# A key-weight load moved to the second DMA queue at the start of a transformer block

## The chip, the cores and the metric

The kernel runs on one core of a Trainium2 chip. Runs e1 to e8 were made on one chip (number 5 in the record) and e9 to e12 on another (number 1); for the first comparison the record names none. Kernels are compared only within the same rounds. The time of a kernel is the device time of one execution in microseconds (us). Most of the time I use the span of the trace, from the first to the last instruction of the program. It is about 1.8 us shorter than the device time of the same execution.

## The reference

A pre-norm block of two halves on `x` of 2048 tokens by 1024 features, in bfloat16:

```
h  = x + LinearAttention(LayerNorm(x)) @ wo      # 32 heads of 32, phi(t) = elu(t)+1
h2 = h + TokenMLP(LayerNorm(h))                  # w1: 2048 -> 3584 tokens, gelu, w2 back
```

The change touches the very beginning only: layer norm of the first token tiles (128 tokens each, called x0, x1, x2, ...), their transposes, and the first products with the key part of `wqkv`.

## The kernel before

The kernel is already tuned, and TensorE (the matmul engine) is its limit: it is busy for 570.0 of 578.6 us. Loads come over two hardware DMA queues, one fed by the sync engine (SP) and one by ScalarE (ACT); nearly everything is on SP's (65.94 MB by the profile page, against 0.13 MB on ACT's). The key weights are loaded as two column blocks, and each block as two halves of 512 KB. "First half" and "second half" below are those of the first block.

```python
            def load_x(i, halves=False):
                x_sb = xload.tile([P, D], BF16, name="x_sb")
                if halves:
                    nc.sync.dma_start(x_sb[:, 0:CW], x[i * P:(i + 1) * P, 0:CW])
                    pin(nc.scalar.dma_start(x_sb[:, CW:D], x[i * P:(i + 1) * P, CW:D]))
                else:
                    nc.sync.dma_start(x_sb[:], x[i * P:(i + 1) * P, :])
                return x_sb
            # ... (cut)
            xs = {0: load_x(0, True)}
            xs[1] = load_x(1)
            for k0 in (0, hk):
                nc.sync.dma_start(wkv[:, k0:k0 + hk, 0:CW], wqkv_v[:, k0:k0 + hk, D:D + CW])
            nc.scalar.add_instruction(  # load of ScalarE's function table
                # ... (cut)
            )
            xs[2] = load_x(2)
            for k0 in (0, hk):
                nc.sync.dma_start(wkv[:, k0:k0 + hk, CW:D], wqkv_v[:, k0:k0 + hk, D + CW:2 * D])
            for i in range(3, G0 + 2):      # x3, x4, x5
                xs[i] = load_x(i)
            # ... the value and query weights follow (cut)
            warm_up(10)                     # matmuls on zeros
            # ... (cut)
            ln_stats(0)                     # VectorE: statistics of x0
            stats(0)                        # ScalarE: rstd of x0
            ln[1] = ln_chunks(1, xs.pop(1))
            pin(ln[1][1](0))                # VectorE: statistics of x1, first half
            norm_halves(0)                  # VectorE: norm of x0 ("norm 0")
            transpose_in(0)                 # TensorE transposes, ScalarE copies
            pin(ln[1][1](1))
            pin(ln[1][2]())
            stats(1)
            k_unit(0, 0)                    # TensorE: x0 times the first key block, 4 + 4 matmuls
            norm_halves(1)
            transpose_in(1)
            ln_stats(2)
            stats(2)
            k_unit(1, 0)
            norm_halves(2)
            # ... k_unit(0, 1) (cut)
            transpose_in(2)
            ln_stats(3)
            # ... rstd of x3 on ScalarE; more work on VectorE (cut)
            norm_halves(3)
            # ... k_unit(1, 1) on TensorE (cut)
            transpose_in(3)
```

`pin` keeps the order of an engine's list as written, and in the traces VectorE runs these instructions in that order. So statistics of x1 that wait for their load also hold up norm 0 behind them.

Of the kernel before, what the change touches and what calls it, by code (L numbers as in the profile page):

```python
# [27 lines left out]
def kernel(  # L28
# [12 lines left out]
    nc = tc.nc  # L41
    x = A_x.flatten_outer_dims()
    o_dram = out.flatten_outer_dims()
    S, D = x.shape
    F = B_w1.shape[1]
    NS, ND, NF = S // P, D // P, F // P
    CW = min(BANK, D)
# [35 lines left out]
    pin = tc.keep_in_program_order  # L83
# [253 lines left out]
    with ExitStack() as actx:  # L337
# [18 lines left out]
        wqkv_v = A_wqkv.rearrange("(k p) c -> p k c", p=P)  # L356
        wo_v = A_wo.rearrange("(k p) c -> p k c", p=P)

        with ExitStack() as a1:
            a1w = a1.enter_context(tc.tile_pool(name="a1w", bufs=1))  # L360
            wkv = a1w.tile([P, ND, 2 * D], BF16)
# [17 lines left out]
# [8 lines that stand above are left out]
# [258 lines left out]
            hk = max(1, ND // 2)  # L645
            assert NDC == 2 and G0 == 4 and ND % 2 == 0
            xs = {0: load_x(0, True)}
            xs[1] = load_x(1)
            for k0 in (0, hk):
                nc.sync.dma_start(wkv[:, k0:k0 + hk, 0:CW], wqkv_v[:, k0:k0 + hk, D:D + CW])  # L650
            nc.scalar.add_instruction(
                mybir.InstLoadActFuncSet(name=nc.get_next_instruction_name(), act_func_set_id=ACT_SET_LN_EXP, ins=[], outs=[])
            )
# [414 lines left out]
```

## Time and profile before

| | before |
|---|---|
| device time, first 3 runs | 579.37 us median (579.31 to 581.21) |
| span of the profiled run | 578.6 us |
| TensorE busy | 570.0 us (99%) |

The first lines of the profile page give the span and the busy time of each engine:

```profile
span 578.6 us, 7489 instructions
...
PE 570.0 (99%) x2832; PEld 267.5 (46%) x2854; DVE 385.6 (67%) x752; ACT 212.6 (37%) x433; POOL 1.8 (0%) x8
```

A table by stretches of time (start:end in us, then busy time and instructions of each engine, granted TensorE clock, DMA share, GB/s) shows where TensorE is not busy:

```profile
0.00:8.27 8.27, 5.30 (x18) 2.02 (x19) 4.61 (x26) 3.20 (x7) 1.83 (x8) 1.00 0.73 234
8.27:18.25 9.98, 8.74 (x55) 4.34 (x56) 7.03 (x17) 6.08 (x16) 0.00 (x0) 1.00 1.09 358
18.25:36.00 17.75, 17.54 (x96) 8.45 (x95) 15.45 (x33) 10.82 (x23) 0.00 (x0) 1.00 0.80 253
```

TensorE (PE) lacks 1.24 us between 8.27 and 18.25 us and 0.21 us in the next stretch. What comes after 18 us is one unbroken piece of matmul work. So the question is when that piece starts.

The timeline of the head (start, duration, engine, line, operation, and in brackets the idle time before it and what ended it):

```profile
5.02 0.64 DVE L396 BATCH_NORM_STATS2 st<-x_sb 128x6 f32<-128x512 bf16 x1
...
5.70 0.73 DVE L406 TENSOR_SCALAR xn<-x_sb,mv,rstd 128x512 bf16<-128x512 bf16 x2
...
6.17 0.85 PE L670 MATMUL tp<-ident,xn 128*128 128x128 bf16 x8 [0.53 <-DVE xn L406]
...
8.27 1.02 PE L427 MATMUL acc_t<-wkv,xnT 128*128 128x512 bf16 x4 [1.25 <-DMA wkv<-in_A_wqkv_dram]
...
9.67 1.02 PE L427 MATMUL acc_t<-wkv,xnT 128*128 128x512 bf16 x4 [0.37 <-DMA wkv<-in_A_wqkv_dram]
...
14.02 1.29 DVE L396 BATCH_NORM_STATS2 st<-x_sb 128x6 f32<-128x512 bf16 x2 [0.79 <-DMA x_sb<-in_A_x_dram]
...
17.28 0.73 DVE L406 TENSOR_SCALAR xn<-x_sb,mv,rstd 128x512 bf16<-128x512 bf16 x2
...
17.75 0.72 PE L670 MATMUL tp<-ident,xn 128*128 128x128 bf16 x8 [0.35 <-DVE xn L406]
```

Line 427 is the product with key weights, line 670 the transposes, line 396 the statistics, line 406 the norm. TensorE waits 1.25 us for the first half of the key weights and 0.37 us for the second. VectorE (DVE) waits 0.79 us for x3 and then works through to norm 3, which releases the transposes of x3 at 17.75 us. TensorE was idle 0.35 us before those. I call the start of these transposes the gate: from there on TensorE hardly waits.

The chain of work that ended last, followed back through the head, agrees: it goes from VectorE's statistics of x3 straight to the DMA of x3 (start, duration, what):

```profile
4.46 9.54 DMA x_sb<-in_A_x_dram
...
14.02 1.30 DVE st L396 x2
```

x3 was issued at 4.46 us and took 9.54 us to land.

### The profile page before, as it was taken

How to read it: one execution, taken by the hardware profiler on the slowest of the kernel's cores; microseconds unless marked ns; L12 is line 12 of the kernel's file. 1: busy time of each engine (PE TensorE's matmuls, PEld its weight loads, DVE VectorE, ACT ScalarE, POOL GpSimd, SP SyncE). 2: the span in 40 equal slices, each digit the busy share in tenths (PEclk: the TensorE clock that was granted, in tenths of full speed). 3: DMA queues.
4: the chain of work that ended last, by engine and by line, in shares of the span. 5: the costliest groups of instructions: out<-in, count | busy, mean ns of one | idle time of the engine just before them, and what ended most of it. 6: DMA issues, size and time to landing. Idle time of an engine off the chain costs nothing.

```text
span 578.6 us, 7489 instructions
## 1 busy us (share of the span) xinstructions
PE 570.0 (99%) x2832; PEld 267.5 (46%) x2854; DVE 385.6 (67%) x752; ACT 212.6 (37%) x433; POOL 1.8 (0%) x8
## 2 busy tenths in 40 slices
PE   7999999999999999999999999999999999999998
PEld 3444444455555444444444444444444444444444
DVE  5898888546767889876666666667765455456443
ACT  4647677666667777342222322222100000000000
POOL 1000000000000000000000000000000000000000
PEclk9999999999999999999999999999999999999999
DMA  8933331029437952152224422203976446431101
GB/s 288 359 81 74 83 81 37 19 88 286 83 73 154 293 171 94 55 146 73 74 72 114 104 74 72 74 0 88 221 218 159 118 126 172 129 99 46 36 28 36
DMA packets 109827, 66.55 MB, mean 115 GB/s; under 512 B 31826, under 2 KB 101728, under 8 KB 109792
## 3 DMA queue, kind: packets, MB, share of 16 engines
q1 hardware_dynamic: 109584, 65.94, 43.0%
q8 instruction: 22, 0.36, 0.3%
q14 instruction: 13, 0.11, 0.1%
q10 hardware_dynamic: 144, 0.13, 0.1%
q0 software_dynamic: 64, 0.01, 0.0%
HBM read 50.34 MB, written 8.39 MB: 102 GB/s over the span
## 4 chain that ended last, share of the span: by engine, by line
PE 93%; DMA 3%; DVE 2%; SPq 1%; issue 1%; ACT 0%; DVEq 0%
PE psZ L228 17%; PE psW L228 17%; PE psX L228 17%; PE acc_t L922 9%; PE acc_t L775 9%; PE psY L228 8%; PE psB L503 4%; PE psC L503 4%; PE psA L503 4%; PE psE L503 2%; DMA x_sb<-in_A_x_dram 2%; PE nd_ps L873 1%; DMA xr<-in_A_x_dram 1%; DVE wo_sb L477 1%; DVE st L396 0%
## 5 line engine op out<-in xcount | busy, mean ns | idle before, releaser
L228 PEld LDWEIGHTS <-sa 128*128 128x128 f16 x1134 | 110.4, 98 | 131.7
L223 DVE TENSOR_TENSOR sa<-w1p 128x1024 f16<-128x1024 bf16 x70 | 47.9, 685 | 20.0 <-PE psX L228 12.4
L775 PE MATMUL acc_t<-xnT,wq_sb 128*128 128x512 bf16 x248 | 57.3, 379 | 0.4
L922 PE MATMUL acc_t<-wo_sb,pqT 128*128 128x512 bf16 x250 | 55.7, 379 | 0.3
L223 DVE TENSOR_TENSOR sa<-w2p 128x1792 f16<-128x1792 bf16 x40 | 43.3, 1084 | 10.1 <-PE psW L228 7.6
L922 PEld LDWEIGHTS <-pqT 128*128 128x128 bf16 x256 | 24.8, 98 | 29.0
L775 PEld LDWEIGHTS <-wq_sb 128*128 128x128 bf16 x256 | 24.6, 98 | 27.4
L164 DVE TENSOR_SCALAR e_sb<-e_sb 128x512 bf16<-128x512 bf16 x64 | 18.5, 289 | 25.9 <-ACT e_sb L160 25.4
L264 DVE TENSOR_TENSOR tt<-psW,dd 128x512 f32<-128x512 f32 x22 | 15.2, 691 | 29.3 <-PE psW L228 29.2
L228 PEld LDWEIGHTS <-w2p 128*128 128x128 bf16 x224 | 21.9, 98 | 26.4
L228 PEld LDWEIGHTS <-w1p 128*128 128x128 bf16 x224 | 21.9, 98 | 26.4
L259 DVE TENSOR_TENSOR psY<-psX,dd 128x512 f32<-128x512 f32 x22 | 15.4, 699 | 27.5 <-PE psX L228 27.5
L160 ACT ACTIVATE e_sb<-acc_t 128x512 bf16<-128x512 f32 x40 | 23.9, 597 | 26.6 <-PE acc_t L775 23.7
L503 PEld LDWEIGHTS <-xs 128*128 128x128 f16 x208 | 20.0, 98 | 23.4 <-DVE xs L489 1.3
L269 DVE TENSOR_TENSOR tt<-tt,psZ 128x512 f32<-128x512 f32 x22 | 15.1, 688 | 18.0 <-PE psZ L228 17.9
L228 PE MATMUL psZ<-hT_2227,w1p 128*128 128x512 f16 x112 | 26.8, 379 | 0.0
L503 PE MATMUL psA<-wkv,xnT 128*128 128x512 bf16 x98 | 26.4, 379 | 0.3
L228 PE MATMUL psW<-hE,sa 128*128 128x512 f16 x112 | 26.6, 379 | 0.0
L228 PE MATMUL psX<-hT_2226,sa 128*128 128x512 f16 x112 | 26.6, 379 | 0.0
L228 PE MATMUL psX<-hO,sa 128*128 128x512 f16 x112 | 26.5, 379 | 0.0
L228 PE MATMUL psW<-hT_2228,w1p 128*128 128x512 f16 x112 | 26.5, 379 | 0.0
L228 PE MATMUL psZ<-hO,sa 128*128 128x512 f16 x112 | 26.5, 379 | 0.0
(258 smaller groups left out, 839.5 us busy)
## 6 DMA issues: line engine op xcount, KB each, us to landing
w1p<-in_B_w_dram SPq DMA_DIRECT2D x14, 1024.0 KB, 5.7
w2p<-in_B_w_dram SPq DMA_DIRECT2D x8, 1792.0 KB, 8.6
xr<-in_A_x_dram SPq DMA_DIRECT2D x16, 256.0 KB, 3.6
x_sb<-in_A_x_dram SPq DMA_DIRECT2D x15, 256.0 KB, 3.0
wkv<-in_A_wqkv_dram SPq DMA_DIRECT2D x4, 512.0 KB, 8.1
wkv<-in_A_wqkv_dram SPq DMA_DIRECT2D x2, 1024.0 KB, 10.0
wq_sb<-in_A_wqkv_dram SPq DMA_DIRECT2D x2, 1024.0 KB, 12.3
wo_sb<-in_A_wo_dram SPq DMA_DIRECT2D x2, 1024.0 KB, 6.6
```

What stands on the lines that cost most here:

```text
L160: pin(nc.scalar.activation(e_sb[:], src, ACT.Exp))
L164: pin(nc.vector.tensor_scalar(e_sb[:], e_sb[:], 1.0, PHI_EPS, ALU.min, ALU.add))
L223: return nc.vector.tensor_tensor(t, a, b, op)
L228: nc.tensor.matmul(ps[:, cols], lhsT=sa[:, k, :], rhs=mv(k)[:, cols], start=(start and k == 0), stop=(stop and k == self.nk - 1), skip_gro ...
L259: nc.vector.tensor_tensor(self.Y[:], self.X[:], self.d[:], ALU.add)
L264: nc.vector.tensor_tensor(self.t[:], self.W[:], self.d[:], ALU.add)
L269: nc.vector.tensor_tensor(self.t[:], self.t[:], self.Z[:], ALU.subtract)
L477: pin(nc.vector.tensor_tensor(out, a, b, ALU.subtract))
L503: pin(nc.tensor.matmul(ps[:], lhsT=lhs[:, k, :], rhs=rhs[:, k, :], start=(start and k == 0), stop=(k == hk2 - 1), skip_group_check=True,))
L775: nc.tensor.matmul(qp[:, 0:SW], lhsT=wq_sb[:, kt, j * P:(j + 1) * P], rhs=xnT[:, kt, u * SW:(u + 1) * SW], start=(kt == 0), stop=(kt == ND ...
L873: nc.tensor.matmul(nd_ps[:, b, sl * NCOL:(sl + 1) * NCOL], lhsT=pqT[:, j, i * P:(i + 1) * P], rhs=ndrhs[:, j, :], start=True, stop=True,)
L922: nc.tensor.matmul(ap_[:, 0:CW], lhsT=pqT[:, j, i * P:(i + 1) * P], rhs=wo_sb[:, j, dc * CW:(dc + 1) * CW], start=(j == 0 and not SEED_RES ...
```

## The change

The intent is to have the first half of the key weights travel beside x1 instead of behind it, so that the first key matmul does not wait. No instruction is added or removed; TensorE's and VectorE's lists stay in the same order.

```diff
             xs[1] = load_x(1)
-            for k0 in (0, hk):
-                nc.sync.dma_start(wkv[:, k0:k0 + hk, 0:CW], wqkv_v[:, k0:k0 + hk, D:D + CW])
+            pin(nc.scalar.dma_start(wkv[:, 0:hk, 0:CW], wqkv_v[:, 0:hk, D:D + CW]))
+            nc.sync.dma_start(wkv[:, hk:ND, 0:CW], wqkv_v[:, hk:ND, D:D + CW])
```

## The prediction

> **What bounds the kernel now.** The page has TensorE busy for 570.0 of 578.6 us (99%). By a table of stretches it is busy 5.30 of the first 8.27 us, 8.74 of the next 9.98, 17.54 of the 17.75 up to 36.0 and over 99% after that; the view of waits lists 0.3 and 0.2 us for it after 18 us. So the kernel ends as much earlier as TensorE reaches its unbroken stretch (from 17.75 us) earlier.
>
> **The head of the kernel (timeline, landing events).** x0 lands at 3.6 to 3.7 us, x1 at 4.6, the first key half block at 8.15, the second at 9.6, x2 at 10.3, x3 at 14.0. TensorE waits 1.2 us for the first half (starts 8.27; ScalarE has copied the transposed x0 at 7.89, its first half at 7.35) and 0.4 us for the second (9.67). VectorE waits 0.8 us for x3, then works without a gap to the end of norm 3 (17.69), which releases the transposes of x3 at 17.75 after 0.35 us of TensorE idle. That is the last gate. Of the first half's 16 engine shares, 15 land by 6.54 us, one at 8.14: one DMA engine took 1.09 us for one 1 KB packet at 4.64, just after its x1 share, and stays 1.4 us behind in every later load (x3: 15 shares by 12.62, the last at 13.99). From 4.0 to 4.5 us the DMA engines moved 59 KB, against 175 KB per half us later.
>
> **What the change does.** No work is added or removed; TensorE's and VectorE's orders stay. ScalarE's queue gets one issue (0.4 to 0.5 us) ahead of its table load (1.28 us); its first real work is at 5.14, so this is free. The sync queue's later issues move forward 0.43 us.
>
> [...] As an estimate from the steady 350 GB/s, x1 shares with at most its own 256 KB of weights and lands up to 0.7 us later, at 4.7 to 5.3. VectorE asks for it at 5.02, ahead of norm 0, so 0 to 0.3 us may be lost there. The first half lands at 6.5 to 7.5, the second at 7.5 to 9. The first key matmul moves from 8.27 to about 7.5, and the 1.6 us of waits for key weights mostly go.
>
> **What reaches the end.** The bytes ahead of x3 are the same, and x3 gates norm 3. x3 gains the 0.1 to 0.4 us by which the slow start is filled; if the straggling engine's stall is hidden behind the other queue, up to about 1.2 us. If x1 is hurt more, zero or a small loss. I put 0.6 us on the end: 578.8 us, range 577.6 to 580.0. Faster by over 2%: 0.01; within 2%: 0.98; slower: 0.01.
>
> **What would show it.** The first matmul on key weights at 7.3 to 7.8 us; x1's stats at 5.0 to 5.4; waits for key weights under 0.6 us; TensorE idle before the transposes of x3 over 0.35 us unless x3 lands earlier; x3 landing at 12.7 to 13.9 and the last TensorE stretch shifted with it.
>
> **What would make it wrong.** Weights not interleaved evenly (x1 after 5.5 us, so norm 0 late); the straggler coming again, on another load; later waits (0.3 us at 36.3) absorbing the gain. Run-to-run noise (579.31 to 581.21) is as large as the effect.

The forecast is 0.6 us off the 579.37 us of the first runs, 578.8. The estimate for x1 (256 KB at the 350 GB/s of the trace, 0.7 us) takes it that x1 and the weights share the engines evenly. That was my assumption; the trace had no two large loads on two queues.

## The result

Six runs of each kernel: 579.7 us median (578.98 to 580.74) after, 580.2 us (579.31 to 581.26) before. The ratio is 0.9992, with a 95% interval of 0.9974 to 1.001. Ratios in this document are the mean time of one kernel's fast runs over that of the other's of the same rounds, so they are not quite the ratios of the medians quoted. By time alone the change is a gain of half a microsecond that noise could also make.

The traces are sharper than the times. The profiled run of the changed kernel has a span of 577.5 us, with 569.7 us of it TensorE's:

```profile
0.00:8.27 8.27, 5.45 (x20) 1.93 (x21) 4.65 (x26) 2.71 (x5) 1.84 (x8) 1.00 0.80 265
8.27:18.25 9.98, 9.38 (x60) 4.73 (x60) 7.99 (x19) 7.62 (x20) 0.00 (x0) 1.00 1.09 357
```

TensorE did 0.64 us more work in the second stretch, though the whole program has the same instructions as before: more of them now fall into this stretch. The timeline of its head:

```profile
1.16 0.45 ACTq L649 DMA_DIRECT2D wkv<-in_A_wqkv_dram  x1
...
5.84 0.69 DVE L396 BATCH_NORM_STATS2 st<-x_sb 128x6 f32<-128x512 bf16 x1 [0.72 <-DMA x_sb<-in_A_x_dram]
6.45 0.72 DVE L406 TENSOR_SCALAR xn<-x_sb,mv,rstd 128x512 bf16<-128x512 bf16 x2
...
6.91 0.72 PE L670 MATMUL tp<-ident,xn 128*128 128x128 bf16 x8 [1.26 <-DVE xn L406]
...
7.98 1.90 PE L427 MATMUL acc_t<-wkv,xnT 128*128 128x512 bf16 x8 [0.36 <-ACT xnT L680]
...
12.50 1.28 DVE L396 BATCH_NORM_STATS2 st<-x_sb 128x6 f32<-128x512 bf16 x2
...
16.21 0.74 DVE L406 TENSOR_SCALAR xn<-x_sb,mv,rstd 128x512 bf16<-128x512 bf16 x2 [0.36 <-ACT rstd L403]
...
16.68 0.72 PE L670 MATMUL tp<-ident,xn 128*128 128x128 bf16 x8
```

The waits for key weights are gone: the eight matmuls run in one go from 7.98 us. VectorE has no idle time before the statistics of x3. The gate is at 16.68 us, 1.07 us earlier, and TensorE's idle time there is down from 0.35 to 0.10 us (too short to be printed). The span fell by 1.1 us. The chain still names x3, but now its landing coincides with VectorE's getting ready for it:

```profile
3.88 8.60 DMA x_sb<-in_A_x_dram
...
12.50 1.30 DVE st L396 x2
```

There is also something bad here. The statistics of x1 waited 0.72 us for x1 (before, they ran at 5.02 us without waiting for it), so norm 0 came at 6.45 instead of 5.70 us, and the transposes of x0 at 6.91 instead of 6.17.

The two traces alone do not tell which of these differences belongs to the change. That is what the experiments are for.

### The profile page after: what moved, and what is told of

Read it like the earlier page. It is cut to its first block, busy times and chain, and to the rows that moved or that the text cites. A ratio compares the mean times of both kernels' runs of the same rounds, so it can differ in the third digit from the quotient of the medians.

```text
span 577.5 us, 7489 instructions
## 1 busy us (share of the span) xinstructions
PE 569.7 (99%) x2832; PEld 267.3 (46%) x2854; DVE 385.8 (67%) x752; ACT 212.9 (37%) x433; POOL 1.8 (0%) x8
## 4 chain that ended last, share of the span: by engine, by line
PE 95%; DVE 2%; DMA 1%; issue 1%; SPq 0%; ACT 0%
PE psW L228 17%; PE psZ L228 17%; PE psX L228 17%; PE acc_t L922 10%; PE acc_t L775 9%; PE psY L228 8%; PE psB L503 4%; PE psC L503 4%; PE psA L503 4%; PE psE L503 2%; PE acc_t L427 1%; DMA x_sb<-in_A_x_dram 1%; PE nd_ps L873 1%; DVE wo_sb L477 1%; DVE st L396 0%
```

## The experiments

All twelve kernels gave the reference's result. A table of what their heads did stands after the first four; it is read from each trace's timeline and from the landing events of the loads (each of these loads shows 16 of them, called its shares; the page counts 16 DMA engines, but the traces do not name the engine behind a share, so the "straggling engine" is read from the last share alone, in the first trace 1.4 us behind the one before it in load after load). A load is waited for to its last share: in the first trace the median share of x3 landed at 12.23 us, the last at 13.99, and the statistics of x3 began at 14.02. A share that lands long after the others is called a straggler.

### Both kernels again (e1, e2, and later e9)

Edit: none. The kernel before (e1):

> The kernel before, unchanged, for a second trace and for the noise of the comparison. If the straggling DMA engine belongs to the order of the loads, it is again there: one of the 16 shares of the first key half lands more than 1 us after the other fifteen, x3 lands at 13.8 to 14.2 us and the transposes of x3 start at 17.6 to 17.9. If it is chance, the lag differs by more than 0.5 us from 1.4, and with it x3. Ratio of times 1.000, and its interval shows what the noise allows (about 0.1%).

The changed kernel (e2):

> The changed kernel, unchanged. If the first trace was typical: x1 lands at 5.7 to 6.0 us (before: 4.4), the first key half within 0.2 us of it, x3 at 12.3 to 12.7, transposes of x3 at 16.6 to 16.8, span 1.0 to 1.2 us under that of the kernel before, ratio 0.998. If the smaller lag of the straggler (0.86 instead of 1.4 us) was chance, x3 can land up to 0.6 us later than in the first trace.

Measured: e1 against the kernel before, which is the same code, ratio 1.000 (0.9985 to 1.0015). e2: 578.99 us median, ratio 0.9988 (0.997 to 1.0006). Both expectations failed in their details. In e1 the first half landed at 6.55 us without a long straggler; the lag of about 1.1 us arose one load later and in two shares. In e2 the gate came 0.8 us before the expected time (the span was 1.0 us under e1's, as expected). x1 was not late: it landed at 4.32 us, and the straggler was almost gone. The lines of e1 that show where it waited:

```profile
7.51 1.04 PE L427 MATMUL acc_t<-wkv,xnT 128*128 128x512 bf16 x4 [0.35 <-ACT xnT L680]
...
8.91 1.02 PE L427 MATMUL acc_t<-wkv,xnT 128*128 128x512 bf16 x4 [0.36 <-DMA wkv<-in_A_wqkv_dram]
...
13.14 1.29 DVE L396 BATCH_NORM_STATS2 st<-x_sb 128x6 f32<-128x512 bf16 x2 [0.67 <-DMA x_sb<-in_A_x_dram]
...
16.87 0.72 PE L670 MATMUL tp<-ident,xn 128*128 128x128 bf16 x8 [0.24 <-DVE xn L406]
```

The timeline of e2:

```profile
4.97 0.64 DVE L396 BATCH_NORM_STATS2 st<-x_sb 128x6 f32<-128x512 bf16 x1
...
5.65 0.73 DVE L406 TENSOR_SCALAR xn<-x_sb,mv,rstd 128x512 bf16<-128x512 bf16 x2
...
6.12 0.72 PE L670 MATMUL tp<-ident,xn 128*128 128x128 bf16 x8 [0.59 <-DVE xn L406]
...
7.20 1.90 PE L427 MATMUL acc_t<-wkv,xnT 128*128 128x512 bf16 x8 [0.35 <-ACT xnT L680]
...
11.68 1.29 DVE L396 BATCH_NORM_STATS2 st<-x_sb 128x6 f32<-128x512 bf16 x2
...
15.89 0.72 PE L670 MATMUL tp<-ident,xn 128*128 128x128 bf16 x8
```

The chain of e2 no longer passes through the loads of x3 or x1 at all. It runs over norm 3, ScalarE's rstd and copies and TensorE's own work back to x0:

```profile
0.74 2.76 DMA x_sb<-in_A_x_dram
...
7.20 1.90 PE acc_t L427 x8
...
10.00 3.63 PE acc_t L427 x16
```

### The software queue, and the table load (e3, e4)

e3, the two small bias loads taken from GpSimd's queue:

```diff
-    nc.gpsimd.dma_start(b1_rows[:], B_b1.rearrange("(t p) -> t p", p=P))
-    nc.gpsimd.dma_start(b2_rows[:], B_b2.rearrange("(t p) -> t p", p=P))
 ...
             for i in range(3, G0 + 2):
                 xs[i] = load_x(i)
+            # the same two loads, from nc.sync
```

> The changed kernel with the two small bias loads (28 and 16 rows of 256 B) moved from the GpSimd queue to the sync queue behind x5. Theory that the software queue's loads make one DMA engine late: the 16 shares of each load from the second key half on land within 0.4 us of each other, x3 lands 0.8 us earlier, at about 11.7; the transposes of x3 move by at most 0.1 us, because TensorE already reaches them without a wait. Rival, the lag comes from the first reads of the weights: it stays at 0.8 us or more and nothing moves.

Measured: ratio 1.0001 (0.9984 to 1.0018), last share of x3 0.28 us behind the median one, gate at 16.04 us. It decides nothing: e2, run beside it with the software queue, had a lag of 0.33 us too, so there was no straggler to remove.

e4, the first half issued behind the table load:

```diff
-            pin(nc.scalar.dma_start(wkv[:, 0:hk, 0:CW], wqkv_v[:, 0:hk, D:D + CW]))
             nc.sync.dma_start(wkv[:, hk:ND, 0:CW], wqkv_v[:, hk:ND, D:D + CW])
             nc.scalar.add_instruction(...)   # table load
+            pin(nc.scalar.dma_start(wkv[:, 0:hk, 0:CW], wqkv_v[:, 0:hk, D:D + CW]))
```

> The changed kernel with the first key half issued on ScalarE's queue behind the table load, so about 1.3 us later (at 2.45 instead of 1.16). Theory A, [...] x1 lands at 4.3 to 4.7 as in the kernel before, its stats no longer hold up norm 0 (norm 0 at 5.7), the key half lands at 6.3 to 7.2, the first key matmul starts at 7.3 to 7.5 and TensorE reaches the transposes of x3 0.4 to 0.7 us earlier if x3 lets it. Theory B, [...] x1 lands at 4.8 to 5.6. If x3 is the gate after all, the end moves by less than 0.2 us.

Measured: ratio 0.9982 (0.9966 to 0.9998). But the edit did not do what I meant:

```profile
1.18 1.28 ACT L650 ACT_TABLE_LOAD   x1 [1.18 <-PEq L1052]
...
1.21 0.42 ACTq L653 DMA_DIRECT2D wkv<-in_A_wqkv_dram  x1
```

The issue did not wait for the table load to finish; it ran 0.03 us after it had started. So e4 is the changed kernel with the first half issued 0.02 us behind x1 instead of just ahead of it, and its head is that of e2: x1 at 4.63 us, gate at 15.89 us. Theories A and B are two outcomes of issuing the first half about 1.3 us later: x1 as early as in the kernel before (A), or late all the same (B). Both stay untested.

### The table of heads

Times in us from the start of the span. "Gate" is the start of the transposes of x3.

| kernel | x1 lands | first half lands | x3: median share, last share | first key matmul | gate | span | span - gate |
|---|---|---|---|---|---|---|---|
| before | 4.38 | 8.14 | 12.23, 13.99 | 8.27 | 17.75 | 578.6 | 560.8 |
| before, e1 | 4.42 | 6.55 | 11.94, 13.11 | 7.51 | 16.87 | 577.7 | 560.8 |
| before, e9 | 4.40 | 6.35 | 11.87, 12.97 | 7.32 | 16.72 | 577.5 | 560.8 |
| changed | 5.82 | 5.88 | 11.49, 12.48 | 7.98 | 16.68 | 577.5 | 560.8 |
| changed, e2 | 4.32 | 5.77 | 11.32, 11.65 | 7.20 | 15.89 | 576.7 | 560.8 |
| e3, biases on sync | 4.63 | 5.99 | 11.59, 11.87 | 7.34 | 16.04 | 576.7 | 560.6 |
| e4, behind x1 | 4.63 | 6.05 | 11.64, 11.87 | 7.20 | 15.89 | 576.7 | 560.8 |
| e11 (same loads) | 4.57 | 6.04 | 11.74, 11.93 | 7.33 | 16.03 | 576.8 | 560.8 |
| e12 (same loads) | 4.43 | 5.82 | 11.63, 11.71 | 7.38 | 16.07 | 576.9 | 560.8 |
| e5, one queue | 6.09 | 5.42 | 11.56, 12.14 | 8.46 | 18.05 | 578.9 | 560.8 |
| e6, swapped | 5.75 | 5.86 | 11.38, 12.36 | 8.12 | 17.98 | 578.8 | 560.8 |
| e7, x1 split | 4.3 | 10.75 | 12.63, 14.78 | 10.89 | 21.72 | 582.5 | 560.7 |
| e10, both halves | 4.35 | 7.21 | 11.59, 12.42 | 7.34 | 17.39 | 578.2 | 560.8 |
| e8, dose | 4.74 | 6.19 | 14.55, 15.09 | 7.06 | 18.85 | 581.3 | 562.5 |

Three things stand in this table. First, the last column: over fourteen rows with gates from 15.9 to 21.7 us, span minus gate is the same to 0.1 us, but for e3 (0.2 us less) and e8. Apart from these, whatever the head does up to the gate reaches the end one for one. Second, in the four heads with the loads of the changed kernel (its two looks, e11 and e12), and in e3 and e4 too, the gate comes 8.69 to 8.70 us after the first key matmul. In the three heads of the kernel before it comes 9.36 to 9.48 us after. Third, x3's last share is 1.1 to 1.8 us behind the median share in the kernel before, and 0.1 to 1.0 us behind in the changed one.

### The order without the queue, and the queues exchanged (e5, e6)

e5:

```diff
-            xs[1] = load_x(1)
-            pin(nc.scalar.dma_start(wkv[:, 0:hk, 0:CW], wqkv_v[:, 0:hk, D:D + CW]))
+            nc.sync.dma_start(wkv[:, 0:hk, 0:CW], wqkv_v[:, 0:hk, D:D + CW])
+            xs[1] = load_x(1)
             nc.sync.dma_start(wkv[:, hk:ND, 0:CW], wqkv_v[:, hk:ND, D:D + CW])
```

> The order of the change without the second queue: x0, first key half, x1, second key half, all but half of x0 on the sync queue. Theory Q, the gain comes from the second queue [...]: long 1 KB packets of over 0.8 us come back on one or two engines, x3 lands at 12.8 to 14.0, the transposes of x3 start at 16.8 to 17.8, span as in the kernel before (577.7 to 578.6). Theory O, the order alone does it: no packet over 0.4 us, x3 at 11.6 to 12.5, transposes of x3 at 15.9 to 16.7. In both x1 lands after the key half, at 5.5 to 6.5, and holds up norm 0.

Measured: 581.68 us median, ratio 1.0029 (1.0015 to 1.0044), the first clear loss. Theory Q is wrong about the stalled packets: the longest packet on the weights took 0.64 us, and x3 landed at 12.14 us, early, as theory O has it. Theory O is wrong about the gate, which came at 18.05 us. What cost the time is x1:

```profile
6.11 0.69 DVE L396 BATCH_NORM_STATS2 st<-x_sb 128x6 f32<-128x512 bf16 x1 [1.18 <-DMA x_sb<-in_A_x_dram]
...
8.46 2.80 PE L427 MATMUL acc_t<-wkv,xnT 128*128 128x512 bf16 x8 [0.25 <-ACT xnT L680]
...
18.05 0.72 PE L670 MATMUL tp<-ident,xn 128*128 128x128 bf16 x8
```

The statistics of x1 waited 1.18 us, norm 0 and the transposes of x0 waited behind them. Then the eight key matmuls took 2.80 us instead of 1.90, because the clock was late: the trace's record of it has the first full-clock stretch begin at 10.31 us in this run, against 4.4 to 7.1 us in the other traces but e6 (10.50 us). The clock column of the views does not show this: it counts the time ahead of the first record as full and gives 1.00 for 8.46 to 10.30 us. So a run's listed mean clock of 1.000 does not exclude a late start of full clock. The loss of 0.29% is thus that of a late x1 with a late clock behind it.

e6:

```diff
-            xs[1] = load_x(1)
-            pin(nc.scalar.dma_start(wkv[:, 0:hk, 0:CW], wqkv_v[:, 0:hk, D:D + CW]))
+            xs[1] = xload.tile([P, D], BF16, name="x_sb")
+            pin(nc.scalar.dma_start(xs[1][:], x[P:2 * P, :]))
+            nc.sync.dma_start(wkv[:, 0:hk, 0:CW], wqkv_v[:, 0:hk, D:D + CW])
```

> The two loads of the change with their queues exchanged: x1 on ScalarE's queue, the first key half on the sync queue. Theory Q [...]: as the changed kernel, x1 at 4.2 to 4.8, key half at 5.5 to 6.1, x3 at 11.6 to 12.5, transposes of x3 at 15.8 to 16.7. Theory S, what helps is that 512 KB leave the sync queue: then the sync queue is as loaded as in the kernel before but for x1 (256 KB), stalled packets of over 0.8 us come back and x3 lands at 12.8 to 14.0.

Measured: ratio 1.0008 (0.9991 to 1.0025), with runs of 578.43 to 581.78 us. No packet stalled (theory S fails), but x1 was late in the profiled run, at 5.75 us, and the rest followed as in e5, the late clock included:

```profile
8.12 3.06 PE L427 MATMUL acc_t<-wkv,xnT 128*128 128x512 bf16 x8 [0.25 <-ACT xnT L681]
```

So the same two loads gave x1 at 4.3 to 4.7 us in six looks with x1 on the sync queue (e2, e3, e4, e8, e11, e12), and at 5.8 us in one (the first); and at 5.75 us in the one look with x1 on ScalarE's queue.

### x1 protected by splitting it (e7)

```diff
-            xs[1] = load_x(1)
+            xs[1] = load_x(1, True)      # first half on sync, second on ScalarE's queue
```

> The changed kernel with x1 itself in two halves on the two queues, ahead of the key halves. [...] it lands at 4.1 to 4.5 in any execution. Key half at 5.5 to 6.2. If x3 and TensorE's own work from the first key matmul are what gates, the transposes of x3 stay at 15.8 to 16.1 and the time equals that of the changed kernel without the x1 delay (ratio 0.998 to 0.999).

Measured: 583.44 us median, ratio 1.006 (1.0047 to 1.0074), all six runs over 582.5 us. x1 landed at about 4.3 us in this one look; "in any execution" one look does not show. The weights were late:

```profile
10.89 3.57 PE L427 MATMUL acc_t<-wkv,xnT 128*128 128x512 bf16 x8 [4.05 <-DMA wkv<-in_A_wqkv_dram]
```

The first key matmul waited 4.05 us for its weights. The eight then took 3.57 us instead of 1.90, for the granted clock was half from 9.30 to 16.13 us; part of the loss is the clock's. Between 4.0 and 6.5 us the DMA engines moved 76 to 146 KB per half microsecond, where the changed kernel moved 175 to 198 (its first trace and e2). I did not expect this and cannot explain it. The loss is no accident of one run, as all six times show; the slow DMA was looked at in one.

### A dose of DMA ahead of x3 (e8)

```diff
+            nc.sync.dma_start(wq_sb[:, :, 0:CW], wqkv_v[:, :, 0:CW])
             for i in range(3, G0 + 2):
                 xs[i] = load_x(i)
 ...
-            for c in range(NDC):
+            for c in range(1, NDC):
                 nc.sync.dma_start(wq_sb[:, :, c * CW:(c + 1) * CW], wqkv_v[:, :, c * CW:(c + 1) * CW])
```

> The changed kernel with 1 MB of query weights loaded ahead of x3 instead of later. A dose for the claim that x3 gates the head and that the head passes one for one to the end: x3 lands 2.9 us later (1 MB at 350 GB/s), at 14.5 to 15.3, the transposes of x3 start 2.2 to 3.0 us later than in the changed kernel (18.0 to 18.9), and the span is 2.0 to 3.0 us longer (578.8 to 579.8), ratio to the kernel before 1.001 to 1.004. Rival, slack later swallows shifts of the head: span within 0.5 us of the changed kernel's 576.7.

Measured: x3 at 15.09 us, gate at 18.85 us, as expected; span 581.3 us, more than expected; ratio 1.0051 (1.0034 to 1.0068). The timeline, with VectorE's wait for x3 and TensorE's for norm 3:

```profile
15.12 1.29 DVE L396 BATCH_NORM_STATS2 st<-x_sb 128x6 f32<-128x512 bf16 x2 [3.62 <-DMA x_sb<-in_A_x_dram]
...
18.85 0.93 PE L671 MATMUL tp<-ident,xn 128*128 128x128 bf16 x8 [3.19 <-DVE xn L406]
```

The gate moved 2.96 us against e2, the span 4.6. The table by stretches (the number before the DMA share is the granted clock) shows the rest:

```profile
16.00:19.14 3.14, 0.29 (x4) 0.23 (x4) 3.00 (x8) 1.47 (x4) 0.00 (x0) 1.00 1.10 349
19.14:22.55 3.41, 3.41 (x13) 1.46 (x12) 1.95 (x6) 2.11 (x4) 0.00 (x0) 0.50 1.10 349
```

After 3.19 us without work TensorE ran 3.41 us at half clock, which costs half of that, 1.7 us: 2.96 + 1.7 = 4.66. All four runs of e8 had a mean granted clock of 0.997, which is what one such stretch makes (3.41 times 0.5 over 581 is 0.003).

### A third look at the kernel before, and both halves on ScalarE's queue (e9, e10)

> The kernel before once more, one look, for a third trace of its head. If the stalled 1 KB packets belong to its order of loads: at least one packet of over 0.8 us between 4 and 7.5 us, one to three shares of x3 over 0.9 us behind the median share, x3 at 13.0 to 14.1, transposes of x3 at 16.8 to 17.8. If they are chance (absent here), x3 lands at 12.2 or earlier and the transposes of x3 start by 16.5.

Measured: packets of 0.77 and 0.72 us (under the 0.8 I had named), x3 at 12.97 us with a lag of 1.1 us, gate at 16.72 us. Taken together, packets of over 0.7 us on x and weights up to 9 us were seen 1, 3 and 2 times in the three looks at the kernel before, and never in the other eleven traces, e5 with its single queue included. The limit of 0.7 was drawn after the traces were seen, and the longest packet elsewhere took 0.69 us (x1 in e8, x0 in e12). So these stalls were seen with the order "weights behind x1 on the sync queue" alone; that this order makes them is likely, not shown. They are also not the only source of a lag: the first trace of the changed kernel has none, and its x3 still ends 1.0 us behind its median share.

e10:

```diff
-            nc.sync.dma_start(wkv[:, hk:ND, 0:CW], wqkv_v[:, hk:ND, D:D + CW])
+            pin(nc.scalar.dma_start(wkv[:, hk:ND, 0:CW], wqkv_v[:, hk:ND, D:D + CW]))
```

> Both key halves on ScalarE's queue beside x1 and x2. If relieving the sync queue is what helps, more of it helps a little: x3 lands at 11.3 to 11.9, transposes of x3 at 15.8 to 16.0, ratio 0.998. If the slow start seen with four loads queued on ScalarE's and the sync queue before the weights (split x1) comes from several pending loads on ScalarE's queue, the key halves land after 7 us, the first key matmul starts after 8 us, and the time is 1 to 4 us over that of the changed kernel.

Measured: 579.51 us median, ratio 1.000 (0.9987 to 1.0013). Neither case came as stated. The first half landed at 7.21 us and the second only at 9.53:

```profile
7.34 1.02 PE L427 MATMUL acc_t<-wkv,xnT 128*128 128x512 bf16 x4 [0.75 <-DMA wkv<-in_A_wqkv_dram]
...
9.57 1.02 PE L427 MATMUL acc_t<-wkv,xnT 128*128 128x512 bf16 x4 [1.21 <-DMA wkv<-in_A_wqkv_dram]
```

The wait for the second half is 1.21 us, so the gain of the changed kernel is lost again. Moving more to the second queue was not better here.

### Filling TensorE's gaps, and VectorE's order (e11, e12)

e11:

```diff
-            warm_up(10)
+            warm_up(11)
 ...
-            transpose_in(0)
+            transpose_in(0); warm_up(1)
```

> The changed kernel with one more warm-up matmul before the transposes of x0 and one after them, in gaps of TensorE of 0.4 us each. Theory that the spread of times comes from stretches of half clock after the gaps of the head: fewer runs with a mean granted clock of 0.997 or less (changed kernel 3 of 12, kernel before 8 of 28), none of 6, and a mean 0.2 to 0.5 us under the changed kernel's; every run under 579.6 us. Rival, the half-clock stretches have nothing to do with these gaps: 1 to 3 of 6 runs at 0.997 and the same mean.

Measured: five runs of 578.42 to 578.65 us, none at 0.997, ratio 0.9984 (0.9973 to 0.9996). The spread is 0.23 us, against 2.7 us over the changed kernel's twelve runs (3 of them at 0.997) and 2.4 us over the 39 runs of the kernel before that are listed with their clock (9 of them at 0.997 or less). This fits the theory, but five runs without a slow one are no proof when three in twelve have one, and the changed kernel did not run in the same rounds nor on this chip. There the kernel before had 1 of 11 runs at 0.997, against 8 of 28 on the other chip, and five of the six runs of e12, without the extra matmuls, lie within 0.13 us. So the steadiness may be the chip's. Against the kernel before the interval of e11 lies under 1, as that of e4 does (0.9966 to 0.9998); whether e11 beats the changed kernel stays open.

e12:

```diff
-            pin(ln[1][1](0))
             norm_halves(0)
+            pin(ln[1][1](0))
```

> The changed kernel with VectorE's norm of x0 ahead of the first stats of x1. The loads are those of the changed kernel, so this is also one more look at them: x1 at 4.3 to 4.7 as in four of its five looks, or near 5.8 as in one. In the first case VectorE's order does not matter: norm 0 at 5.0 to 5.7 (it waits for ScalarE's rstd), stats of x1 0.7 us later than before, TensorE's transposes of x1 up to 0.5 us later, time within 0.3 us of the changed kernel. In the second case the first key matmul starts at 7.1 to 7.4 instead of 7.98.

Measured: 578.6 us median, ratio 0.9992 (0.9977 to 1.0006); five runs at 578.55 to 578.68 us and one at 581.01 us with a clock of 0.997. x1 was on time (4.43 us), so VectorE's order did not matter, as the first case has it. The second case, the one this edit is for, did not come up.

## Why the prediction was right, and where its steps were not

The predicted 578.8 us and its range (577.6 to 580.0) held the measured 579.7, and "within 2%" was right. But the range would have held no change at all (579.37 us in the runs then known), so the number proves little about the steps. Point by point:

**What bounds the kernel: right, and better than I had claimed.** Span minus gate is 560.7 to 560.8 us in all but two of the rows. Of the exceptions, e8 adds a clock penalty that I had not thought of; the 0.2 us of e3 are unexplained.

**Waits for key weights mostly go: right.** They are zero in every trace with the changed loads. But the 1.25 us wait for the first half, which the change is named after, was special to the first trace. In e1 and e9 the first key matmul waited for ScalarE's copy, not for weights (7.51 and 7.32 us), and the kernel before then waited only 0.36 and 0.27 us, for the second half. So the first key matmul gains little: mean 7.70 us in the three looks at the kernel before, 7.59 us in the two at the changed one (7.20 to 7.38 us in e3, e4, e11 and e12, which have nearly the same loads).

**x3 gains 0.1 to 0.4 us, up to 1.2 if the straggler's stall is hidden: mis-sized.** The last share of x3 landed at 13.36 us in the mean of three looks before, and at 11.94 us in the mean of the four heads with the changed loads: 1.4 us earlier. Of that, 0.5 us is the median share (12.01 to 11.55), the slow start filled (from 4.0 to 4.5 us the DMA engines moved 59 KB in the first trace before, 198 KB in the first changed one and 193 KB in e2); 0.9 us is the lag of the last share behind the median (1.34 to 0.40); the stalled packets that are no longer seen fit this part, but what keeps them away is open.

**What reaches the end: right in kind.** After the first key matmul the changed kernel needs 8.7 us to the gate, by e2's chain for TensorE's own work, ScalarE's copies and rstd, and norm 3. The kernel before added its wait for the second half (0.37, 0.36, 0.27 us) and its idle time before the transposes of x3 (0.35, 0.24, 0.38 us), 0.66 us in the mean. In the changed kernel the first is zero and the second 0.1 us. The gate moved from 17.11 us (three looks) to 16.29 us (two), 0.8 us, where I put 0.6. x3 landing any earlier than it now does gives nothing: in e2 the chain does not pass through it.

**x1 lands up to 0.7 us later, at 4.7 to 5.3: wrong, both ways.** In six of seven looks it lands at 4.3 to 4.7 us, 0.1 us earlier to 0.3 us later than before. In one it is 1.4 us later and holds up norm 0; the prediction had named this ("x1 after 5.5 us") among what would make it wrong. Two loads issued 0.01 to 0.04 us apart on two queues did not share the engines evenly. In e2, from 3.0 to 3.5 us, the sync queue had 84 packets of x1 under way and ScalarE's queue was finishing x0; in the first trace of the changed kernel in that time ScalarE's queue ran 146 packets and the sync queue 2 of x1. What no run shows is which of the two had work ready at the engines, so this start says nothing of how they choose between queues. In a stretch in which both queues were well under way the shares were nearly even: in e10 from 7.5 to 8.0 us, 91 packets of the sync queue and 87 of ScalarE's. I also misread a number: the landing at 4.6 us that I gave to x1 before was that of a bias load; x1 landed at 4.4.

**What the second queue brought.** Not more data per time: between 4.0 and 4.5 us e2 moved 193 KB, all of it from ScalarE's queue, and e5 188 KB from the sync queue (and 6 KB of the bias loads). What it bought is order: in six of seven looks the weights went early without holding up x1. e5 shows what early weights in front of x1 cost, 0.29%. The time went both ways with what was on which queue: one queue with weights first 1.0029, the second queue 0.9992 and 0.9988 (1 is within both intervals), both halves on it 1.000, x1 split over both 1.006.

**Why the times show so little.** The mean spans of the traces differ by 0.8 us (577.9 before, 577.1 changed), the medians of the first six runs by 0.5. Each kernel's runs spread over 2.4 to 2.7 us, more than the effect. Part of the spread goes with the granted clock: the nine runs of the kernel before at 0.997 or less have a mean of 580.72 us, the other thirty 579.56 (the changed kernel's nine others 579.07, half a microsecond less). But eight of these thirty had spans of 576.9 to 577.2 us, between those of the changed kernel's two traced runs. As an estimate from span minus gate, 560.8 us, their gates were at 16.1 to 16.4 us: the kernel before at times has a head as early as the changed one's, which none of its three traces caught, and the 0.8 us is an estimate from few looks. As to the clock, the half-clock stretch of e8 lasted 3.41 us, that of e7 6.83. e8's began 0.29 us after a TensorE gap of 3.19 us, e7's 2.46 us into one of 4.05. At the start, after 4.45 us of warm-up matmuls, TensorE had gaps of 1.54 us in e5 and 1.19 us in e6 before the transposes of x0, and the record of full clock began at 10.31 and 10.50 us only. In the first trace of the changed kernel it began at 5.53 us; a gap of 1.26 us (5.65 to 6.91) came just after, and the clock stayed full. That the gaps made the clock late in e5 and e6, and that gaps of the head also cause the half-clock stretches of runs without a trace, is argued, not shown.

**Open.** Why single packets stall for 0.7 to 1.4 us when the weights stand behind x1 on one queue; which of two loads issued together goes first (in the one look in which x1 lost on the sync queue, ScalarE had issued 0.04 us ahead of it, in the others 0.01 to 0.02 us ahead or behind, which one look cannot make a rule); why e7 slows the DMA down for 2.5 us.

## What to carry to other kernels

When an engine is busy without a break after some point, find the one instruction at which that begins and compare its start between traces: here span minus gate was the same to 0.2 us (but for one kernel with a late half-clock stretch), while six timed runs could not tell 0.8 us. Two or three looks at each kernel are needed first, because the beginning of this kernel differed by a microsecond from one execution to the next (gates of 16.72 to 17.75 us in three looks), and the most visible wait of a single trace (1.25 us here) may be absent in the next. The second DMA queue was here a tool for order, not for speed, and not a sure one (x1 lost in one of seven looks): put on it what is needed early and must not delay what is needed first, and no more than that.
